# Crossbar DMA transposes of whole row blocks issued from ScalarE, in place of TensorE transposes of x and half-block transposes from SP

## The chip, the core and the metric

The kernel runs on one core of one Trainium2 chip. The metric is the device time of one execution in microseconds (us). The span of a profiled execution is some 2 us shorter than its time (1463.0 of 1464.76 us before). Several executions were timed for each kernel, and comparisons use the fast ones alone. A single-core run has no second die to compare with, so a run is called slow when it is over 1.5% above the fastest of the same kernel.

## The reference, cut to what matters

x has 8 batches, 4224 tokens and 192 channels. A causal convolution of seven taps along the tokens is followed by a token and channel mixer:

```python
theta = x @ w_theta
zr, zi = x * cos(theta), x * sin(theta)
y = einsum('ts,bsd->btd', w_tok_r, zr) + einsum('ts,bsd->btd', w_tok_i, zi)
u = x + y
out = u + maximum(u @ w_ch, 0)
```

The two 4224 x 4224 token matrices are nearly all of the work. The kernel makes the two 192 x 192 channel products (`x @ w_theta`, `u @ w_ch`) from x and u with channels on the partitions, so it transposes both. These transposes are what the change is about.

## The kernel before: the parts that the change touches

The 4224 source tokens lie in 33 chunks of 128. A step makes two blocks of 128 output tokens from the 11 chunks (9 or 10 at times) that are in memory, with seven Strassen-like runs of big matmuls for the pair. Partial sums of the outputs go to DRAM and come back one pass later. Everything is placed by hand: an event has a position in its step, counted in runs, called units here (about 3.6 us each).

Chunks 0 to 10 are prepared at the start. Chunks 11 to 21 and 22 to 32 are prepared inside running steps, one or two in a step; I call these the chunk steps of the first and second pass. The last 17 steps finish the outputs.

```python
def crossed(u):                        # crossbar transpose by DMA, half a block, from SP
    uT = turned()                      # [P, 6, P] float16, 4 buffers
    nc.sync.dma_start(out=uT, in_=u, transpose=True)
    return uT

def transposed(u, by_dve=False):       # six 128x128 transposes on TensorE, copied out of PSUM
    tp = banks("tp", F16)
    for k in range(6):
        pe(nc.tensor.transpose(tp[:, 0, k*P:(k+1)*P], u[:, k*P:(k+1)*P], ident))
    uT = turned()
    evacuate(...)                      # ScalarE (VectorE for a few)
    return uT

# Chunk.tasks: conv, conv, transpose, transpose, theta, theta, product, product, sums, sums
pos = [0, .5, 1.3, 1.6, 2.1, 2.5, 3.1, 3.15, 3.4, 3.6]     # units; the second chunk 2.3 later

# output rows: cast u to float16 (ScalarE), transpose (crossbar; TensorE in the last steps), mix
every, turn, mix = 3.6, 1.7, 9.0                            # us
```

GpSimd issues the loads of weights and x, which change float32 to float16 on the way (the software queue, q0: 163616 packets in the page of the kernel before). SP issues the partial sums in 6144-byte packets, the stores of x and the outputs (q1: 109648 packets).

## Time and profile before

| | before |
|---|---|
| time, median of the runs beside the changed kernel | 1470.94 us (1464.91 to 1472.31, 4 runs) |
| span of the profiled run | 1463.0 us |
| TensorE busy / idle | 1418.8 / 44.2 us |
| granted TensorE clock, mean | 0.998 |
| TensorE's waits for transposed x / u | 0 / 6.2 us |

TensorE is busy nearly all the time, so time is lost only where it waits, and gained only where it has less to do. The two windows below, from the windows view of the kernel before, hold the chunk steps of both passes. Their columns: window, length, busy us and instructions of PE, PEld, DVE, ACT and POOL, granted clock, DMA share, GB/s.

```profile
400.00:640.00 240.00, 239.27 (x1747) 150.18 (x1746) 172.86 (x195) 72.96 (x92) 66.85 (x119) 1.00 0.98 225
860.00:1110.00 250.00, 247.02 (x1819) 156.33 (x1818) 189.34 (x208) 77.54 (x98) 76.15 (x116) 1.00 0.96 211
```

TensorE is idle for 0.7 us in the first window and 3.0 us in the second. The DMA share is near 1, but shares of packets that overlap add up, so 1 isn't a ceiling of this share: the prediction shows a stretch of 1.16.

### The profile page before, as it was taken

The numbers are of one execution on the slowest core, as the hardware profiler recorded it, in microseconds if no ns is written. First come the engines' busy times: TensorE is split into PE (matmuls) and PEld (weight loads), VectorE is DVE, ScalarE is ACT, GpSimd is POOL, SyncE is SP. The second block draws the span as 40 slices with busy tenths as digits, with TensorE's granted clock in tenths as the row PEclk, the third lists the DMA queues.
The fourth block names the chain that finished last, engine by engine and source line by source line (L and its number), as shares of the span: only waits on it lengthen the run. The fifth ranks groups of instructions, "written<-read, shape, count | busy, mean of one in ns | idle before, by whom it ended". The sixth has DMA issues, their size and how long they took to land.

```text
span 1463.0 us, 23889 instructions
## 1 busy us (share of the span) xinstructions
PE 1418.8 (97%) x9807; PEld 886.8 (61%) x9807; DVE 992.6 (68%) x1050; ACT 324.2 (22%) x413; POOL 429.2 (29%) x659
## 2 busy tenths in 40 slices
PE   7889999999999999999999999999999999998997
PEld 4556666666666666666666656666566666665565
DVE  6884645454548687766666657877787788776676
ACT  6861111111124254000000005346001100110134
POOL 7422211111223332211112233232233343454210
PEclk9999999999999999999999999999999999999999
DMA  9976757474699999977779989999899999999994
GB/s 172 217 167 147 143 97 152 88 152 94 133 236 222 213 244 250 199 212 153 217 152 227 227 174 238 192 222 251 178 207 214 224 224 217 221 265 234 223 216 139
DMA packets 273374, 283.57 MB, mean 194 GB/s; under 512 B 107504, under 2 KB 241008, under 8 KB 273264
## 3 DMA queue, kind: packets, MB, share of 16 engines
q0 software_dynamic: 163616, 95.30, 49.0%
q1 hardware_dynamic: 109648, 186.75, 40.2%
q8 instruction: 77, 1.26, 0.3%
q14 instruction: 33, 0.27, 0.1%
HBM read 245.49 MB, written 111.28 MB: 244 GB/s over the span
## 4 chain that ended last, share of the span: by engine, by line
PE 80%; DVE 8%; DMA 5%; ACT 3%; issue 2%; POOL 0%; SPq 0%; DVEq 0%; ACTq 0%; POOLq 0%
PE y L417 72%; PE v L138 5%; DVE pv L382 2%; ACT z L242 2%; DVE wt L317 2%; DVE wt L329 2%; DMA out_dram<-pv 1%; PE pc L205 1%; PE tp L162 1%; DVE pv L446 1%; DMA uT<-ub 1%; DVE z L253 1%; DMA xw<-in_x_dram 1%; DVE z L247 1%; DMA st<-in_moe_w_tok_r_dram 1%
## 5 line engine op out<-in xcount | busy, mean ns | idle before, releaser
L417 PE MATMUL y<-z,wt 128*128 128x384 f16 x7656 | 1289.4, 326 | 10.9 <-DVE pv L382 10.0
L417 PEld LDWEIGHTS <-wt 128*128 128x128 f16 x7656 | 739.7, 98 | 485.6 <-issue 15.2
L382 DVE TENSOR_TENSOR pv<-y,pv 128x768 f32<-128x768 f32 x324 | 308.2, 952 | 362.3 <-PE y L417 333.9
L317 DVE STREAM_TRANSPOSE wt<-st 128x1408 f16<-128x1408 f16 (+7 forms) x224 | 326.4, 1462 | 26.6 <-PE y L417 19.7
L304 POOL DMA_DIRECT2D st<-in_moe_w_tok_i_dram x232 | 132.6, 580 | 496.8 <-DVE wt L317 463.3
L304 POOL DMA_DIRECT2D st<-in_moe_w_tok_r_dram x232 | 133.6, 598 | 436.4 <-DVE wt L317 421.2
L329 DVE TENSOR_TENSOR wt<-wt 128x1408 f16<-128x1408 f16 (+7 forms) x216 | 196.1, 908 | 21.8 <-PE y L417 18.2
L148 ACT ACTIVATE z<-pc 128x768 f16<-128x768 f32 x65 | 52.9, 813 | 386.6 <-PE pc L205 386.5
L436 ACT ACTIVATE ub<-pv 128x768 f16<-128x768 f32 x66 | 53.7, 838 | 349.7 <-DVE pv L382 271.8
L380 ACT ACTIVATE pv<-y 128x768 f32<-128x768 f32 x66 | 53.6, 813 | 281.6 <-PE y L417 281.6
L138 PEld LDWEIGHTS <-uT 128*128 128x128 f16 x1056 | 91.0, 98 | 32.3 <-issue 8.8
L192 POOL DMA_DIRECT2D xw<-in_x_dram x132 | 76.2, 586 | 34.4 <-DMA st<-in_moe_w_tok_r_dram 10.9
L446 DVE SCALAR_TENSOR_TENSOR pv<-v,pv 128x768 f32<-128x768 f32 x66 | 62.3, 946 | 27.6 <-PE v L138 20.9
L148 ACT ACTIVATE uT<-tp 128x768 f16<-128x768 f16 x79 | 63.3, 813 | 65.9 <-PE tp L162 65.9
L253 DVE TENSOR_TENSOR z<-z 128x768 f16<-128x768 f16 x132 | 73.3, 555 | 3.8
L364 POOL TENSOR_TENSOR pv<-pv,xr 128x1536 f32<-128x1536 f32 x20 | 62.8, 3138 | 30.6 <-DMA xr<-xs 22.2
L242 ACT ACTIVATE z<-v,half_pi 128x768 f16<-128x768 f32 x66 | 59.5, 902 | 41.7 <-PE v L138 41.6
L247 DVE TENSOR_TENSOR z<-z 128x1536 f16<-128x1536 f16 x66 | 60.3, 949 | 11.7 <-ACT z L242 11.7
L138 PE MATMUL v<-wch,uT 128*128 128x192 f16 x528 | 54.3, 246 | 8.6 <-DMA uT<-ub 6.2
L138 PE MATMUL v<-wth,uT 128*128 128x192 f16 x528 | 55.0, 248 | 3.1 <-ACT z L242 3.0
L242 ACT ACTIVATE z<-v 128x768 f16<-128x768 f32 x66 | 53.1, 805 | 0.0
L162 PE MATMUL tp<-ident,z 128*128 128x128 f16 x396 | 33.0, 220 | 8.5 <-ACT z L242 8.0
(43 smaller groups left out, 157.3 us busy)
## 6 DMA issues: line engine op xcount, KB each, us to landing
part<-pv SPq DMA_DIRECT2D x79, 768.0 KB, 4.3
pv<-part SPq DMA_DIRECT2D x79, 768.0 KB, 5.6
out_dram<-pv SPq DMA_DIRECT2D x66, 384.0 KB, 5.9
st<-in_moe_w_tok_r_dram POOLq DMA_DIRECT2D x136, 176.0 KB, 6.2
st<-in_moe_w_tok_i_dram POOLq DMA_DIRECT2D x136, 176.0 KB, 4.9
xs<-z SPq DMA_DIRECT2D x132, 96.0 KB, 4.6
xw<-in_x_dram POOLq DMA_DIRECT2D x121, 96.0 KB, 6.1
part<-xs POOLq DMA_DIRECT2D x26, 384.0 KB, 8.8
```

Source lines behind the costliest of these rows:

```text
L138: pe(nc.tensor.matmul(v[:, k, b * D : (b + 1) * D], lhsT=tT[:, 3 * k + b + i, :], rhs=w[:, 2 * b + i, :], start=(i == 0), stop=(i == 1),))
L148: act(nc.scalar.activation(out=out, in_=in_, func=AT.Copy))
L192: nc.gpsimd.dma_start(out=self.xw[lo : lo + n, h, :, :], in_=x[:, t0 : t0 + n, :].rearrange("b s d -> s b d"),)
L242: act(nc.scalar.activation(**args))
L247: dve(nc.vector.tensor_tensor(out=o, in0=xv, in1=o, op=ALU.mult))
L253: dve(nc.vector.tensor_tensor(out=z[:, o, :], in0=z[:, a, :], in1=z[:, b, :], op=ALU.subtract))
L304: pool(nc.gpsimd.dma_start(out=st[a * Q : (a + 1) * Q, 0:nb, :, 0:n] .rearrange("i r bt s -> i (r bt) s"), in_=w[self.tbs[0] * P : (self.t ...
L317: dve(nc.vector.transpose(self.w[name][:, 0 : self.n, :, :], self.st[int(name[1])][:, int(name[0]) - 1, :, 0 : self.n * Q] .rearrange("p b ...
L329: dve(nc.vector.tensor_tensor(out=self.w[name][:, 0 : self.n, :, :], in0=self.w[a][:, 0 : self.n, :, :], in1=self.w[b][:, 0 : self.n, :, : ...
L382: dve(nc.vector.tensor_tensor(out=o, in0=yv, in1=o, op=ALU.add))
L417: pe(nc.tensor.matmul(y[cn][:, q, 0:BH], lhsT=self.w[wn][:, c, :, :].rearrange("p bt i -> p (bt i)"), rhs=chunks[k].z[:, zn, q * BH : (q + ...
L446: dve(nc.vector.scalar_tensor_tensor(out=ub, in0=channel_mix(self.uT[i, g], wch), scalar=0.0, in1=ub, op0=ALU.max, op1=ALU.add,))
```

## The change

The intent: take the transposes of chunks 11 to 32 off TensorE, issue all crossbar transposes for whole blocks (128 x 1536) from ScalarE right behind the copies that make their source, and give them more time by placing theta later.

```diff
     def turned():
-        return wk.tile([P, 6, P], F16, name="uT", tag="uT", bufs=4)
+        return wk.tile([P, 12, P], F16, name="uT", tag="uT")
-    def crossed(u):
-        uT = turned()
-        nc.sync.dma_start(out=uT, in_=u, transpose=True)
+    def crossed(uT, u, by_sp=False):
+        if by_sp:
+            nc.sync.dma_start(out=uT, in_=u, transpose=True)
+        else:
+            act(nc.scalar.dma_start(out=uT, in_=u, transpose=True))
 ...
+        def cross(self):
+            self.xT = turned()
+            crossed(self.xT, self.x, self.k < NW)
 ...                                    # Chunk.tasks
-            for g in range(NG):
-                yield lambda g=g: self.transpose(g)
+            yield self.cross
 ...
-            return wpool.tile([P, NW, NQ, Q], F16, name="wt", tag="wt", bufs=10)
+            return wpool.tile([P, NW, NQ, Q], F16, name="wt", tag="wt", bufs=9)
 ...                                    # outputs of the steps that are not the last
-                    at = (8.5 if i else 0.9 - self.time / 7) if self.pair else 0.7
-                    every, turn, mix = 3.6, 1.7, 9.0
+                    at = (4 if i else 0.9 - self.time / 7) if self.pair else 0.7
+                    for g in range(NG):
+                        found.append((at + g, lambda i=i, g=g: self.cast(i, g)))
+                        found.append((at + 10.5 + 2.8 * g, lambda i=i, g=g: self.output(i, g)))
+                    found.append((at + 2, lambda i=i: self.cross_u(i)))
 ...                                    # places of a chunk's tasks
-                pos = [0, .5, 1.3, 1.6, 2.1, 2.5, 3.1, 3.15, 3.4, 3.6]
+                pos = [0, .4, .9, 4, 4.4, 5, 5.05, 5.25, 5.45]
-                at += 2.3
+                at += 0.9
```

More of the change, by code (lines that the diff above doesn't have):

```diff
@@ L150, in turned, with transposed @@
     def turned():
-        return wk.tile([P, 6, P], F16, name="uT", tag="uT", bufs=4)
-    def crossed(u):
-        uT = turned()
-        nc.sync.dma_start(out=uT, in_=u, transpose=True)
-        return uT
-    def transposed(u, by_dve=False):
+        return wk.tile([P, 12, P], F16, name="uT", tag="uT")
[4 more added lines that the diff above has]
+            act(nc.scalar.dma_start(out=uT, in_=u, transpose=True))
+    def transposed(uT, u, by_dve=False):
         tp = banks("tp", F16)
@@ L164, in transposed @@
             ))
-        uT = turned()
-        evacuate(uT[:, :, :].rearrange("p k s -> p (k s)"), tp[:, 0, 0 : 6 * P], by_dve)
-        return uT
+        evacuate(uT.rearrange("p k s -> p (k s)"), tp[:, 0, 0 : 6 * P], by_dve)
     Z11, T1, Z21, Z22, T2, T4, T3 = range(7)
@@ L175, in __init__ @@
             self.k = k
-            self.xT = {}
             self.xw = wk.tile([2 * WR, 2, B, D], F16, name="xw", tag="big", bufs=6)
@@ L226, in transpose @@
         def transpose(self, g):
-            self.xT[g] = transposed(
-                self.x[:, g * GC : (g + 1) * GC], 0 < self.k < 3 or (self.k, g) == (0, 1)
-            )
+            if g == 0:
+                self.xT = turned()
+            transposed(
+                self.xT[:, 6 * g : 6 * g + 6, :], self.x[:, g * GC : (g + 1) * GC],
+                0 < self.k < 3 or (self.k, g) == (0, 1),
+            )
+        def cross(self):
+            self.xT = turned()
+            crossed(self.xT, self.x, self.k < NW)
         def theta(self, g):
-            v = channel_mix(self.xT[g], wth).rearrange(
+            v = channel_mix(self.xT[:, 6 * g : 6 * g + 6, :], wth).rearrange(
                 "p k (b h e) -> p k b h e", b=2, h=2
@@ L434, in cast, with cross_u @@
         def cast(self, i, g):
-            self.ub[i, g] = wk.tile([P, GC], F16, name="ub", tag="ub", bufs=2)
+            if g == 0:
+                self.ub[i] = wk.tile([P, N], F16, name="ub", tag="ub", bufs=2)
+                self.uT[i] = turned()
+            cols = slice(g * GC, (g + 1) * GC)
             act(nc.scalar.activation(
-                out=self.ub[i, g], in_=self.pv[i][:, g * GC : (g + 1) * GC], func=AT.Copy
+                out=self.ub[i][:, cols], in_=self.pv[i][:, cols], func=AT.Copy
             ))
         def turn_u(self, i, g):
-            self.uT[i, g] = (transposed if self.late else crossed)(self.ub[i, g])
+            transposed(
+                self.uT[i][:, 6 * g : 6 * g + 6, :], self.ub[i][:, g * GC : (g + 1) * GC]
+            )
+        def cross_u(self, i):
+            crossed(self.uT[i], self.ub[i])
         def output(self, i, g):
@@ L446, in output @@
             dve(nc.vector.scalar_tensor_tensor(
-                out=ub, in0=channel_mix(self.uT[i, g], wch), scalar=0.0, in1=ub,
+                out=ub, in0=channel_mix(self.uT[i][:, 6 * g : 6 * g + 6, :], wch), scalar=0.0, in1=ub,
                 op0=ALU.max, op1=ALU.add,
@@ L459, in outputs @@
             for i in range(len(self.tbs)):
-                if self.late:
-                    at = 1.2 if i or not self.pair else 0.6 - self.time / 7
-                    every, turn, mix = 2.0, 1.2, 3.6
-                else:
-                    at = (8.5 if i else 0.9 - self.time / 7) if self.pair else 0.7
-                    every, turn, mix = 3.6, 1.7, 9.0
+                if not self.late:
+                    at = (4 if i else 0.9 - self.time / 7) if self.pair else 0.7
+                    for g in range(NG):
+                        found.append((at + g, lambda i=i, g=g: self.cast(i, g)))
+                        found.append((at + 10.5 + 2.8 * g,
+                                      lambda i=i, g=g: self.output(i, g)))
+                    found.append((at + 2, lambda i=i: self.cross_u(i)))
+                    continue
+                at = 1.2 if i or not self.pair else 0.6 - self.time / 7
+                every, turn, mix = 2.0, 1.2, 3.6
                 for g in range(NG):
```

## The prediction

> **What bounds the kernel now.** I read the page first (parts 1, 2, 4 and 5), then the engines in 50 us windows, then the timeline of one step in which later chunks of x are prepared, then who the TensorE waited for, then the DMA view.
>
> ```profile
> PE 1418.8 (97%) x9807; PEld 886.8 (61%) x9807; DVE 992.6 (68%) x1050; ACT 324.2 (22%) x413; POOL 429.2 (29%) x659
> L417 PE MATMUL y<-z,wt 128*128 128x384 f16 x7656 | 1289.4, 326 | 10.9 <-DVE pv L382 10.0
> L148 ACT ACTIVATE uT<-tp 128x768 f16<-128x768 f16 x79 | 63.3, 813 | 65.9 <-PE tp L162 65.9
> L162 PE MATMUL tp<-ident,z 128*128 128x128 f16 x396 | 33.0, 220 | 8.5 <-ACT z L242 8.0
> ```
>
> The TensorE is busy for 1418.8 of 1463.0 us, so only 44 us are idle, and about 20 of those lie in the first 100 us, which the change leaves alone. Whatever takes work off the TensorE shortens the kernel, unless a wait takes its place. The transposes of x (L162, 396 of them = 66 half blocks of six) are such work. ScalarE, at 22%, is not a bound.
>
> The busy times of short matmuls overlap their neighbours, so I take their real cost from the starts in the timeline of the TensorE:
>
> ```profile
> 454.57 0.65 PE L417 MATMUL y<-z,wt 128*128 128x384 f16 x3
> 455.06 0.50 PE L162 MATMUL tp<-ident,z 128*128 128x128 f16 x6
> 455.39 1.14 PE L417 MATMUL y<-z,wt 128*128 128x384 f16 x6
> 456.37 0.50 PE L162 MATMUL tp<-ident,z 128*128 128x128 f16 x6
> 456.70 0.33 PE L417 MATMUL y<-z,wt 128*128 128x384 f16 x1
> ```
>
> Six transposes hold the array for 455.39 - 455.06 = 0.33 us (again 456.70 - 456.37), not for the 0.50 us shown as busy. A big matmul takes (456.37 - 455.39)/6 = 0.163 us. So a half block costs 0.33 us, or 55 ns a transpose.
>
> The waits of the TensorE between 1300 and 1400 us, and the windows of a chunk step, a plain step, a final step and a stretch near the end (columns: length, busy us of PE, PEld, DVE, ACT, POOL with counts, clock, DMA share, GB/s):
>
> ```profile
> PE v L138 <- DMA uT<-ub: 6.2, 5, 2.1
> 441.50:468.20 26.70, 26.70 (x217) 17.22 (x216) 22.36 (x27) 12.66 (x16) 9.10 (x16) 1.00 1.04 235
> 650.00:675.00 25.00, 25.00 (x156) 15.07 (x154) 16.17 (x16) 0.00 (x0) 4.55 (x8) 1.00 0.77 184
> 1089.00:1117.20 28.20, 27.84 (x189) 17.71 (x187) 22.12 (x20) 3.26 (x4) 10.84 (x11) 1.00 1.03 219
> 1312.00:1360.00 48.00, 42.27 (x286) 26.43 (x284) 29.72 (x31) 4.11 (x5) 24.08 (x28) 1.00 1.16 226
> ```
>
> The chunk steps and most final steps have a full TensorE; only around 1312 to 1360 us is time lost (5.7 us), nearly all of it to crossbar transposes of u that land late. VectorE is at 22.36/26.70 = 84% in a chunk step, and the DMA share is already about 1.0 there.
>
> [...] In this trace a TensorE transpose inside a stream costs 55 ns, so I use that. [...] on SP a transpose issued at 1083.34 us moved its first packet only at 1086.74, while 6144-byte packets of a partial-sum transfer were passing. [...]
>
> **The change part by part.**
> (a) x of the chunks 11 to 32. Removed from the TensorE: 22 chunks x 2 half blocks x 0.33 us = 14.5 us. All of it lies in windows where the TensorE is 100% busy (about 430 to 590 and 880 to 1050 us), so it comes off the end one for one. ScalarE loses 44 copies of 0.81 us and gains 22 DMA issues. An issue of half a block took 1.25 us on SP, so I estimate 2.5 us for a whole one: 36 us less, 55 us more, at an idle engine. The PSUM buffers that the next convolution and theta need are two deep, and no more than one is held up behind an issue, so I charge nothing.
> (b) Does the transpose land in time? It is placed 0.9 and theta 4.0 units of a step (a seventh, some 3.6 us) after the chunk's start: 3.1 x 3.6 = 11.2 us. In the packet records a half-block transpose is 768 packets of 256 bytes, 18 ns each undisturbed; alone it spans 0.9 us from first to last packet, beside other queues 2 to 2.7 us in the 1077 to 1260 us stretch. The first packet comes 1.2 us after the issue. For a whole block: copy and semaphore 1, first packet 1.2, 1536 packets 2 to 6 us, so 4 to 8 us, under 11.2. Charge: 0, with some risk of 1 or 2 us in a few chunks.
> (c) DMA load. 1536 x 18 ns / 16 = 1.7 us of all engines per chunk; 11 chunks in about 155 us add 0.12 to the share of 1.0. The stretch from 1312 us ran at 1.16, and there transfers were late; the one from 1089 ran at 1.03 without waits for transfers. Weights and partial sums are asked for some 20 us ahead, so I charge 1 us.
> (d) The VectorE bunches. Before, the products and sums of a step's two chunks stood at 3.2 to 3.7 and 5.5 to 6.0 units; now at 5.1 to 5.55 and 6.0 to 6.45. A chunk takes two products and four sums, by starts in the timeline 1.74 + 2.24 = 4.0 us. From unit 5.0 the VectorE has: addition of the fifth product 0.88, weight sum 0.67, chunk 4.0, addition of the sixth 0.88, chunk 4.0, addition of the seventh 0.88 = 11.3 us. The last must be done when run 0 of the next step ends, at unit 8.0, 3.0 x 3.55 = 10.65 us later, for the accumulator is reused then. It misses by some 0.6 us. The kernel before shows this wait in one such bunch:
>
> ```profile
> 496.70 3.57 PE L417 MATMUL y<-z,wt 128*128 128x384 f16 x21 [0.73 <-DVE pv L382]
> ```
>
> There are five two-chunk steps in each of two passes: 10 x 0.6 = 6 us lost.
> (e) u. 48 half-block transposes on SP become 24 whole ones on ScalarE, which no longer queue behind the transfers of SP. Their distance from the first cast to the first use grows from 9.0 to 10.5 us, but the first half now waits for the whole. Undisturbed steps had no wait and gain nothing. Near the end the half blocks' packets spanned 4 to 6.5 us each beside accumulating transfers, so a whole block (2 us until it is issued, 1.2, then 8 to 10) is still late by 1 to 2 us there, two or three times. Of the 6.2 us lost I expect 3 to come back.
> (f) One weight tile fewer. Counting live tiles through a step (seven in use, freed one per run; eight made), the most is nine, reached at units 2.2, 3.05, 3.3, 4.2 and 5.1, each just after a run has freed one. The VectorE has waited for that run anyway. Charge 0.
> Sum: -14.5 + 1 + 6 - 3 = -10.5 us on 1463, so 0.7%. On the median 1470.62 that is 1460; since the runs before scatter from 1464.91 to 1471.26 with the median at the upper end, I put 1458.
>
> **The rivals.** (1) No new wait: the VectorE slips by less than I worked out and all late transposes vanish. Then -14.5 - 6 - 2 = -22 us, about 1446. For it: the margin in (d) is a difference of nearly equal numbers. Against: 84% VectorE already. (2) The crossbar transpose of x becomes the wait: at a DMA share of 1.13, whole blocks take 10 us or more, theta waits 1 or 2 us in each of 22 chunks (theta's slack is 3 to 7 us), so 22 to 40 us are lost against 14.5 gained: 1475 to 1490. For it: the bursts of 4 to 6.5 us near the end. Against: those stood beside accumulating transfers, which chunk steps lack. (3) The saved array time is hidden, because a step is paced by the VectorE (84%, 88% after a step shortened to 25.4 us): gain only 2 to 4 us, about 1467. For it: (d). Against: a queue at 88% with one run of slack follows most of the shortening.
>
> **Range and chances.** Rival 1 sets the low edge, rival 3 with a mild form of 2 the high one: 1445 to 1471. Over 2% faster would need 29 us, more than the 14.5 + 6.2 us plus the small VectorE waits on offer: 4%. Over 2% slower needs rival 2 in full: 3%. Within 2%: 93%.
>
> **What would show each step right or wrong.** L162 down from 396 to 132 on z, PE busy down by 14 to 22 us (22 because busy time counts overlap): (a). TensorE waits on the transposed x near zero: (b); several us in total: rival 2. TensorE waits for L382 in the chunk windows near 6 us: (d); near 0: rival 1. Waits of v for the transposed u at 2 to 4 us after 1300: (e). VectorE waits for the TensorE at the weight tiles unchanged near 20 to 40 us: (f). Chunk steps about 1.3 us shorter, or 0.7 with the waits of (d). What would make all of it wrong is a wait on ScalarE's sequencer, which now issues DMAs between copies: if an issue blocks it for far over 2.5 us, convolutions and sines stand behind it.

Its sum came to -10.5 us (-14.5 + 1 + 6 - 3).

## The result, and the profile after

The changed kernel takes 1561.93 us (median of 4 runs, 1543.7 to 1571.47), against 1470.94. The ratio is 1.0536, with a 95% interval of 1.0461 to 1.0611. Ratios here are the mean time of one kernel's fast runs over that of the other's in the same rounds, so they are not quite the ratio of the medians quoted. The kernel became 5% slower where a gain of 1% had been predicted. It also scatters more: two of its four runs are over 1.5% above its fastest and count as slow. The profiled run (1553.38 us, span 1551.3) is a fast one.

First the page of the changed kernel, which answers the lines in the prediction (L421 is the old L417):

```profile
PE 1431.6 (92%) x9543; PEld 884.2 (57%) x9543; DVE 1006.9 (65%) x1050; ACT 289.4 (19%) x369; POOL 430.3 (28%) x659
...
PEclk9999999999999999999999988998999999988999
...
L138 PE MATMUL v<-wth,uT 128*128 128x192 f16 x528 | 59.7, 261 | 43.1 <-DMA uT<-z 40.6
L138 PE MATMUL v<-wch,uT 128*128 128x192 f16 x528 | 56.2, 251 | 31.6 <-DMA uT<-ub 30.0
```

The view of groups shows the transposes left of x:

```profile
L163 PE MATMUL tp<-ident,z 128*128 128x128 f16 x132 | 11.7, 230 | 8.2 <-ACT z L247 7.6 <-ACT z L148 0.5
```

The work did leave TensorE: 396 transposes of x became 132. Yet its busy time rose, from 1418.8 to 1431.6 us, and its idle time rose from 44.2 to 119.7 us. The row PEclk, the granted clock in tenths, has new dips in the columns where the idle time is. The waits of TensorE in the changed kernel (total us, times, longest):

```profile
PE v L138 <- DMA uT<-z: 40.6, 8, 11.1
PE v L138 <- DMA uT<-ub: 30.0, 7, 15.4
PE y L421 <- DVE pv L386: 10.9, 11, 3.6
...
PE pc L203 <- DMA xw<-xw: 6.2, 5, 2.9
PE pc L203 <- DMA xw<-in_x_dram: 5.9, 3, 3.1
```

and the one of VectorE before:

```profile
PE y L417 <- DVE pv L382: 10.0, 15, 1.8
```

70.6 us are waits for transposes, where the kernel before had 6.2. Another 12.1 us are waits of the convolution for the loads of x. The wait for VectorE, from which I had expected the main loss, hardly moved. The same windows as above, with one near the end:

```profile
400.00:640.00 240.00, 216.19 (x1477) 131.73 (x1475) 160.63 (x182) 57.00 (x71) 64.61 (x114) 0.97 1.10 224
860.00:1110.00 250.00, 217.06 (x1440) 131.58 (x1439) 160.16 (x182) 52.98 (x67) 64.03 (x112) 0.92 1.06 198
1360.00:1410.00 50.00, 34.61 (x216) 21.52 (x215) 24.31 (x24) 3.15 (x4) 16.32 (x18) 0.83 1.20 191
```

TensorE issues fewer matmuls in the same windows and gets a clock of 0.83 to 0.97. What that means for one matmul is seen in the timelines just after a wait, first the weight loads:

```profile
452.38 0.15 PEld L421 LDWEIGHTS <-wt 128*128 128x128 f16 x1 [0.17 <-issue]
452.69 0.15 PEld L421 LDWEIGHTS <-wt 128*128 128x128 f16 x1 [0.17 <-issue]
453.01 0.15 PEld L421 LDWEIGHTS <-wt 128*128 128x128 f16 x1 [0.17 <-issue]
```

and the matmuls, eight in a row each:

```profile
450.80 1.46 PE L138 MATMUL v<-wth,uT 128*128 128x192 f16 x8 [7.59 <-DMA uT<-z]
452.05 2.67 PE L421 MATMUL y<-z,wt 128*128 128x384 f16 x8
```

After a wait of 7.59 us the big matmuls follow each other every 0.32 us instead of 0.163. The clock records of the trace agree: they show 12 stretches at exactly half clock between 100 and 1500 us, of 3.41 to 17.07 us and all whole multiples of 3.41 us, all at waits of about 3 us and more (12 of the 13 waits of 2.88 us or more are followed by one); the kernel before has none between 100 us and its last matmul.

This gives the account of the 88.3 us between the two spans. TensorE's idle time grew by 119.7 - 44.2 = 75.5 us. The overlap of the half-clock stretches with busy TensorE time is 50.8 us, half of which, 25.4 us, is lost. The transposes saved 14.5 us. Together 75.5 + 25.4 - 14.5 = 86.4 us; some 2 us are left over.

By stage, I take the times from the start of the 2000th big matmul to that of the 3200th (it holds the first pass's chunk steps), from the 4700th to the 6000th (the second pass's), and from there to the end:

| span, us | first pass | second pass | end |
|---|---|---|---|
| before | 230.1 | 257.4 | 334.7 |
| after | 252.6 | 298.8 | 357.2 |
| loss | 22.5 | 41.4 | 22.5 |

Between these stages the two kernels are alike (243.8 us both), and the first 2000 matmuls take 1.9 us longer after.

Lateness shows in the view of the transposed tile, between 890 and 1090 us of the changed kernel (durations of an issue in ns, then issue to landing):

```profile
L158 ACTq DMA_TRANSPOSE uT<-z x11: 1383/1678/6583, 900.9 to 1067.2; - x11
...
DMA to landing us min/median/max: 3.2/7.4/21.2
```

I had allowed 11.2 us. In the packet records, the 1536 packets of one whole-block transpose of x span between 1.55 and 16.22 us. The two shortest (1.55 and 1.77 us) have no packets of the software queue beside them. The longest, issued at 905.38 us, has 1647 data packets of that queue and 128 of 6144 bytes beside it. Issuing can block ScalarE's sequencer as well, as this timeline near the end shows:

```profile
1373.59 19.09 ACTq L158 DMA_TRANSPOSE uT<-ub  x1
1394.41 1.46 PE L138 MATMUL v<-wch,uT 128*128 128x192 f16 x8 [15.39 <-DMA uT<-ub]
```

One issue holds ScalarE's sequencer for 19.09 us, until just after the transpose before it has landed (its last packet ends at 1391.16).

### The profile page after: what moved, and what is told of

Its sections match the earlier page's. It is cut to its first block, busy times and chain, and to the rows that moved or that the text cites. A ratio compares the mean times of both kernels' runs of the same rounds, so it can differ in the third digit from the quotient of the medians.

```text
span 1551.3 us, 23231 instructions
## 1 busy us (share of the span) xinstructions
PE 1431.6 (92%) x9543; PEld 884.2 (57%) x9543; DVE 1006.9 (65%) x1050; ACT 289.4 (19%) x369; POOL 430.3 (28%) x659
## 3 DMA queue, kind: packets, MB, share of 16 engines
q10 hardware_dynamic: 72128, 18.09, 10.1%
## 4 chain that ended last, share of the span: by engine, by line
PE 69%; DMA 18%; DVE 7%; ACT 4%; issue 2%; POOL 0%; SPq 0%; ACTq 0%; DVEq 0%
PE y L421 62%; DMA uT<-z 7%; DMA uT<-ub 5%; PE v L138 5%; DVE pv L386 2%; DMA st<-in_moe_w_tok_r_dram 2%; DMA xw<-in_x_dram 2%; ACT z L247 1%; DMA xw<-xw 1%; DVE z L252 1%; PE pc L203 1%; DVE z L258 1%; DVE wt L333 1%; DVE pv L458 1%; DVE wt L321 1%
## 5 line engine op out<-in xcount | busy, mean ns | idle before, releaser
L421 PE MATMUL y<-z,wt 128*128 128x384 f16 x7656 | 1298.7, 329 | 11.8 <-DVE pv L386 10.9
L421 PEld LDWEIGHTS <-wt 128*128 128x128 f16 x7656 | 747.4, 99 | 501.9 <-issue 27.7
L321 DVE STREAM_TRANSPOSE wt<-st 128x1408 f16<-128x1408 f16 (+7 forms) x224 | 327.5, 1465 | 42.5 <-PE y L421 36.2
L333 DVE TENSOR_TENSOR wt<-wt 128x1408 f16<-128x1408 f16 (+7 forms) x216 | 204.1, 945 | 45.9 <-PE y L421 43.4
L138 PEld LDWEIGHTS <-uT 128*128 128x128 f16 x1056 | 94.9, 102 | 99.3 <-DMA uT<-z 43.6
L138 PE MATMUL v<-wth,uT 128*128 128x192 f16 x528 | 59.7, 261 | 43.1 <-DMA uT<-z 40.6
L203 PE MATMUL pc<-xw,bands 96*64 96x192 f16 x528 | 38.1, 260 | 14.1 <-DMA xw<-xw 6.2
L203 PEld LDWEIGHTS <-bands 96*64 96x64 f16 x528 | 22.7, 112 | 35.5 <-issue 26.8
```

Of the source, the lines that this page charges most:

```text
L138: pe(nc.tensor.matmul(v[:, k, b * D : (b + 1) * D], lhsT=tT[:, 3 * k + b + i, :], rhs=w[:, 2 * b + i, :], start=(i == 0), stop=(i == 1),))
L203: pe(nc.tensor.matmul(pc[half * 2 * Q : (half + 1) * 2 * Q, h // 2, h % 2 * B * G : (h % 2 + 1) * B * G], lhsT=bands[:, 4 * j + h, :, :].r ...
L321: dve(nc.vector.transpose(self.w[name][:, 0 : self.n, :, :], self.st[int(name[1])][:, int(name[0]) - 1, :, 0 : self.n * Q] .rearrange("p b ...
L333: dve(nc.vector.tensor_tensor(out=self.w[name][:, 0 : self.n, :, :], in0=self.w[a][:, 0 : self.n, :, :], in1=self.w[b][:, 0 : self.n, :, : ...
L421: pe(nc.tensor.matmul(y[cn][:, q, 0:BH], lhsT=self.w[wn][:, c, :, :].rearrange("p bt i -> p (bt i)"), rhs=chunks[k].z[:, zn, q * BH : (q + ...
```

## The experiments

The theories at the start: **A**, the crossbar's small packets take turns with those of the other queues on each DMA engine, so a transpose is late wherever those are busy, whichever queue issues it; **B**, ScalarE's own ring is at fault ("ring" and "row" here and in the expectations mean a queue of the page: in the changed kernel q10 with 72128 packets holds the transposes from ScalarE, beside SP's q1 and the software queue q0); **C**, x alone overloads the DMA engines and u suffers from it; **D**, the whole block is at fault, since theta's first half waits for all of it. After the first four runs **L** came in: the chunk steps have no room left on the DMA engines. By each packet's undisturbed duration, an estimate from the trace's shortest packets of each size, 0.88 of the engines' time is taken between 450 and 560 us of the kernel before, and the transposes of x add 0.12.

The six runs marked "one run" among the kernels were executed once, so their state is unknown, and near-copies of the changed kernel scatter from 1543.7 to 1592.54 us. From single runs I therefore read waits and packets more than the time.

### Parts of the change: u alone and x alone

u_alone: whole-block transposes of u from ScalarE stay, x goes back to TensorE.

```diff
-            yield self.cross
+            for g in range(NG):
+                yield lambda g=g: self.transpose(g)
-                pos = [0, .4, .9, 4, 4.4, 5, 5.05, 5.25, 5.45]
+                pos = [0, .5, 1.3, 1.6, 2.1, 2.5, 3.1, 3.15, 3.4, 3.6]
-                at += 0.9
+                at += 2.3
```

> x of all chunks by TensorE again, at its old places in the step; u in whole blocks from ScalarE as in the changed kernel. The parts of the loss are read from the changed kernel's trace. Theory A (the crossbar's small packets take turns with the packets of the software queue and of SP, so a transpose is late wherever those are busy): the u part stays: the 30 us that TensorE waited for u against 6 before, and some 12 us of half clock after the long waits, so about 1495 us. Theory B (ScalarE's own ring is at fault): the same, about 1495. Theory C (only x overloads the DMA engines, and u is late as a consequence of that): near 1465.

Measured: correct, 1486.26 us (median of 4), ratio 1.0099 (1.0048 to 1.015). The stages are 230.1, 257.2 and 354.9 us: the passes are as before, the end is 20.2 us longer. TensorE waits 26.6 us for u, all of it in three waits between 1285 and 1372 us (the longest 15.8), where the kernel before lost 6.2. So C falls: u is late on its own account. The unchanged passes also show that nine weight tiles cost nothing.

x_alone: x as in the change, u again in half blocks from SP at the old places.

```diff
+                crossed(*half, by_sp=True)      # in turn_u, half a block
-                    at = (4 if i else 0.9 - self.time / 7) if self.pair else 0.7
+                    at = (8.5 if i else 0.9 - self.time / 7) if self.pair else 0.7
+                    every, turn, mix = 3.6, 1.7, 9.0
```

> u in half blocks from SP at its old places again (its cast still goes into a whole-block tile); x by crossbar from ScalarE as in the changed kernel. Theories A and B: the waits for x (40 us), those for the x windows (12 us) and some 20 us of half clock stay, less the 14.5 us of transposes: about 1518 us. Theory C: about 1540, nearly the whole loss.

Measured: correct, 1540.36 us (median of 4), ratio 1.0509 (1.0455 to 1.0563), which is more than A and B expected. Stages 248.9, 307.9, 339.1. TensorE waits 51.1 us for x. The transposes of x make most of the loss, those of u about 20 us, and the two nearly add up. (The transposes from ScalarE end at 1083.71 us and those from SP begin at 1121.66, so the two queues never transpose at the same time here.)

### The ring and the size: all_sp and halves

all_sp issues every crossbar transpose from SP (`if by_sp:` becomes `if True:`).

> The changed kernel with every crossbar transpose issued from SP instead of ScalarE, same sizes and places. Theory B (own ring, starved by turns): the transposes' packets span 2 to 5 us again and the time falls to about 1460. Theory A (turns with the software queue, on either ring): the packets of the late ones still span 8 us or more, and SP's queue adds its own waiting: 1530 to 1580 us.

Measured: correct, 1532.88 us (one run; before 1468.38). Stages 244.9, 300.1, 343.5. The spans of the x transposes' packets fall to 1.6 to 7.4 us, but the first packet comes 1.2 to 6.6 us after the issue (1.2 to 4.8 us in the change). In the kernel before, where SP issues them too, other packets of SP went first: the transpose issued at 1083.34 us had its first packet at 1086.74. TensorE waits 48.7 us for x, in 14 waits of up to 7.0 us. B falls as an explanation of the time: without the ring of its own the spans are shorter but the first packet comes later, and the wait for x (40.6 us in the change) is no less. B did foresee the shorter spans, and A's "8 us or more" was too high there.

halves gives each whole-block transpose as two half-block ones, both from ScalarE:

```diff
-            crossed(self.xT, self.x, self.k < NW)
+            for g in range(NG):
+                crossed(self.xT[:, 6*g : 6*g+6, :], self.x[:, g*GC : (g+1)*GC])
```

(and the same for u).

> The changed kernel with each whole-block transpose given as two half-block ones, one after the other, from ScalarE. Theory D (the whole block is at fault: theta's first half waits for all of it): the waits for x and u fall by more than half, about 1500 us. Theory A: the packets are the same and take the same turns; the first half comes some 4 us earlier but the second is needed only 1.5 us after the first, so the waits fall by a quarter at most: 1530 to 1550 us.

Measured: correct, 1501.41 us (one run). D met its number, and A, which had asked for 1530 to 1550 us, missed. But look at TensorE's waits in this run:

```profile
PE pc L203 <- DMA xw<-in_x_dram: 13.3, 7, 3.8
PE pc L203 <- DMA xw<-xw: 12.4, 10, 3.2
...
PE v L138 <- DMA uT<-z: 4.9, 5, 1.8
```

The wait for the transposed x shrinks from 40.6 to 4.9 us, and that for the loads of the next chunks' x doubles from 12.1 to 25.7. What lands late changed. Stages 241.8, 278.5, 337.1: nearly all of u's loss is gone, and about half of the loss in the two passes stays (11.7 + 21.1 us). The turns themselves are as many as A had them: while the transposes of x ran, 8389 data packets of the software queue and 822 of 6144 bytes went by (7803 and 787 in the change). But they are spread otherwise, and the longest time from a chunk's first issue to its last packet fell from 20.5 to 12.5 us. So a part of the loss goes with the size of the block; whether by the earlier first half or by the shorter worst case, this run doesn't tell.

### Nobody waits for the transposes: dummy

The kernel before, with 22 whole-block transposes in the places of the change that nobody reads:

```diff
+    def unread():
+        dst = wk.tile([P, 12, P], F16, name="dT", tag="xr", bufs=2)
+        act(nc.scalar.dma_start(
+            out=dst, in_=wboth.rearrange("p a d -> p (a d)"), transpose=True))
 ...
+                n_x = sum(1 for j in range(NW, k) if start[j] == start[k])
+                found.append((1.0 + 0.9 * n_x, unread))
```

(`wboth` holds the two channel matrices, 1536 columns; nine weight tiles.)

> The kernel before (x and u as there) plus 22 whole-block crossbar transposes that nobody reads, issued from ScalarE where the changed kernel issues those of x; source and target are tiles that nothing else uses at that time, one weight tile fewer as in the change. Theory L (in the chunk steps the DMA engines have no room left: by undisturbed packet times 0.88 of their time is taken before, and the transposes of x add 0.12): other transfers come late, above all the loads of x for the next chunks, though no instruction waits for a transpose: 1485 to 1520 us. Theory A (only the lateness of the transposes themselves costs): 1463 to 1472 us.

Measured: correct, 1587.61 us (one run; before 1463.7): slower than the change itself and than either theory had it. TensorE still does all transposes of x here and no instruction reads the new ones. In the waits view:

```profile
ACT z L242 <- issue: 86.5, 8, 19.6
...
PE v L138 <- ACT z L242: 66.3, 15, 17.7
```

and in the timeline, where the issue of a transpose stands before ScalarE's next sine:

```profile
468.55 16.50 ACTq L481 DMA_TRANSPOSE dT<-wboth  x1
...
485.10 0.90 ACT L242 ACTIVATE z<-v,half_pi 128x768 f16<-128x768 f32 x1 [15.20 <-issue]
```

The issue takes 16.50 us, and the sine that theta needs stands behind it, so TensorE waits for ScalarE. The semaphore that this issue waits for had its last update at 463.6 us, before the issue began, so the 16.50 us are no wait for a semaphore. This is a second way in which late transposes cost: ScalarE's sequencer is held for as long as an issue takes. In the change it costs little at x, where theta needs the transpose anyway (the longest issue there is 6.58 us). Because of this, dummy doesn't measure the load alone, and L can't be read from it.

### Less traffic: lighter, quiet, no_w

lighter leaves out the stores of partial sums in the chunk steps of the second pass: `if not self.final and not 35 <= self.t <= 40:`.

> The changed kernel with the stores of partial sums left out in the chunk steps of the second pass (steps 35 to 40; wrong results on purpose), which takes away 0.14 of the DMA engines' time there. The first pass is the control and should lose what it lost before (some 25 us of idle TensorE between 430 and 610 us). Theory L: in the second pass TensorE's idle time falls from 34 us (gaps over 1 us between 900 and 1080 us) to under 10. Theory A: the transposes still take turns with the software queue's packets, so at least 20 us stay.

Measured: wrong output, 1540.38 us (one run). Stages 245.8, 290.9, 359.2. The first pass, whose code is that of the change, differs from the change's own profile by 6.8 us, so the 7.9 us by which the second is shorter tell nothing. The windows view for the second pass:

```profile
860.00:1110.00 250.00, 214.81 (x1454) 130.96 (x1453) 160.09 (x182) 55.76 (x70) 62.01 (x109) 0.94 0.98 166
```

The rate fell from 198 to 166 GB/s, and TensorE is as idle as before (250 - 214.81 = 35.2 us against 32.9). L, which asked for gaps under 10 us, missed its forecast. But the DMA share of this window is still 0.98 (1.06 in the change), so the run shows only that leaving out the stores is not enough; it doesn't show that there was room.

quiet was to move the first weight load of a chunk step from 1.3 to 3.4 units, away from the transposes.

> The changed kernel with the first weight load of a chunk step moved from 1.3 to 3.4 units, away from the two transposes of x, nothing taken away. Theory A: the second transposes span 3 to 5 us instead of 8 to 16, waits for x fall from 40 us to under 15, time about 1510. Theory L: the same bytes in the same step; the waits move to other transfers and the time stays at 1535 to 1560.

Measured: correct, 1592.54 us (one run). Neither theory was tested, because the edit did not do what I meant. In the timeline the load is issued at 430.45 us against 431.65 in the change: in both, the idle time of GpSimd before it (12.43 and 12.41 us) was ended by VectorE, which frees the weight buffer, so moving the event did not put the load later. As a nearly unchanged copy the run shows instead how widely such a kernel scatters (1543.7 to 1592.54 us with the change's own runs).

no_w leaves out the weight loads of steps 35 to 42 (issued two steps earlier, so in all chunk steps of the second pass) and uses those of step 34:

```diff
+            if 35 <= self.t <= 42:
+                self.st[m] = steps[self.t - 1].st[m]
+                return
```

> The changed kernel with the weight loads of steps 35 to 42 left out, the weights of step 34 used instead (wrong on purpose): in the steps of the second pass that prepare x, but the last two, the software queue carries only x. The first pass is the control (some 25 us of gaps). Theory A: the second transposes of a step in the second pass span under 6 us instead of 11 to 16 and their waits (24 us between 900 and 1080 us) fall under 5, until the last step or two. If they stay late, taking turns with the weights is not the cause.

Measured: wrong output, 1498.08 us (one run). Its windows view for the first pass (control) and the second:

```profile
400.00:640.00 240.00, 216.72 (x1463) 131.83 (x1462) 159.71 (x182) 56.63 (x71) 63.81 (x112) 0.95 1.11 224
860.00:1110.00 250.00, 245.02 (x1698) 150.88 (x1696) 189.47 (x208) 58.85 (x74) 41.91 (x65) 0.99 0.79 188
```

The control loses 23 us of TensorE as in the change, the second pass 5. There the waits for transposed x are under 1 us in all (24.4 in the change) and the packets span 1.6 to 4.9 us. The stage takes 253.4 us, 4 us less than before the change. So beside x's own loads and all partial sums the change works as it was meant, and beside the weight loads it does not. That is A's forecast. (It takes away bytes too, some 0.33 of the engines' time, as I estimate from the undisturbed durations of the packets; lighter had taken 0.14 without effect, so this pair alone does not exclude a threshold.)

### The cost by itself: micro and micro2

A kernel of its own has phases in which everything is waited for in between: one whole-block transpose alone, or beside weight loads as the kernel issues them, 768 KB loads of partial sums, or both.

> The disputed cost by itself (output wrong on purpose): a whole-block crossbar transpose (1536 packets of 256 bytes) in phases with everything waited for in between: from ScalarE alone; beside two weight loads of the software queue; beside four 768 KB loads of partial sums on SP; beside both; then beside both as two halves, from SP behind its loads, none, and whole from ScalarE and from SP again. Theory A (each DMA engine serves one packet of each row with work in turn): per engine 96 turns, of 18 ns alone, 18+74 beside weights, 18+234 beside sums, 18+74+234 beside both, as long as the neighbours last: spans 1.7 us alone, about 8.8 beside weights, about 9 beside the sums (their 32 packets an engine last 32 turns, 8 us), 12 to 18 beside both; halves the same in sum; from SP it starts only after the loads (8 us or more) and then spans under 9. Theory L (bytes alone count): beside both the transpose ends only 2 us later than alone plus its share, under 6 us.

Measured: 322.66 us, mostly inconclusive. The software queue's first packets come 4 us after the start of a phase, and by then the transposes from ScalarE had ended: 2.00 us from first to last packet alone, 2.00 and 2.01 beside neighbours that had not begun. Later phases overlapped only in part. In micro2, ScalarE therefore copies for some 8 us first, and there are more loads:

```diff
+            for _ in range(5):
+                nc.scalar.activation(out=slow, in_=zero, func=AT.Copy)
+            nc.scalar.activation(out=src, in_=slow, func=AT.Copy)
             cross(nc.scalar, halves)
```

> In micro the transposes had run before the neighbours' transfers began (4 us after the issue), so most phases told nothing. Here ScalarE copies for about 8 us before it issues the transpose, the weight loads are sixteen (some 20 us) and the sums eight, so that the transpose runs amid them (output wrong on purpose). Phases: alone; beside weights; beside sums; beside both; both, as halves; from SP behind four of the sums, weights running; both; weights; sums; both without a transpose. Theory A (one packet of each row in turn): spans 2.0 us alone (as micro showed); 96 x (18+74) = 8.8 us beside weights; 96 x (18+234), cut off when the sums end, so 10 us or more beside sums; more than beside either when beside both, 15 us or more; from SP it starts late and then spans about 8.8. Theory L (room alone): under 5 us beside one neighbour, since neither fills the engines.

Measured (504.35 us for the whole, output wrong), from the packet records:

| phase | span of the 1536 packets | packets of the others in it |
|---|---|---|
| alone | 2.00 us | none |
| beside weights | 8.17 us | 1643 of the weights |
| beside both | 21.86 us | 1639 of the weights, 896 of the sums |
| both, as two halves | 21.86 us | 1682 and 896 |
| weights again | 9.88 us | 1354 |

The DMA view of the window of the second phase says the same (queue, packets, MB, share of the 16 engines; 1536 packets of data and 32 small ones make 1568):

```profile
q0 software_dynamic: 1782, 1.18, 93.5%
q10 hardware_dynamic: 1568, 0.39, 35.5%
```

and of the third, where the partial sums (q1) come in:

```profile
q1 hardware_dynamic: 1008, 5.51, 66.2%
q0 software_dynamic: 1783, 1.18, 36.9%
q10 hardware_dynamic: 1566, 0.39, 11.5%
```

Against A's forecast of 8.8 us beside weights stand 8.17 and 9.88; against "15 us or more" beside both stand 21.86. For each of its 1536 packets about one of the weights' goes by (1643), although they are nearly three times as large. Halves do not change the sum, as A had it. L's "under 5 us" is refuted, and so is its premise that one neighbour doesn't fill the engines: just before the transpose of the second phase began, the weights alone moved 254 packets per us, at a DMA share of 1.26. With the transpose there, between 78 and 84 us, 194 weight packets and 206 of the transpose went by per us. So the transpose did not get what was left over; the weights gave way. Beside both, between 136 and 153 us, the counts per us are 52 of the weights, 49 of the sums and 55 of the transpose, though their packets have 704, 6144 and 256 bytes. In this stretch the three queues shared by packets, and not by bytes. It wasn't always so even: "weights again" met 1354 weight packets, and another phase meant to be beside both met 1047 of the weights, only 37 of the sums, and took 10.50 us. The phases beside sums alone missed the overlap (11 and 9 sum packets), and the transpose from SP ended before the weight loads began, so these say nothing.

The real kernels show the same order. I sorted the half-microseconds within the transposes' spans of six runs with whole blocks from ScalarE (after, u_alone, x_alone, dummy, quiet, lighter) by whether any data packet of the software queue or of SP's queue starts in them. The transposes move 797 packets per us where there is neither, 278 where there are some of the software queue, 330 where there are some of SP, and 119 where there are both. At these mean rates 1536 packets take 1.9, 5.5, 4.7 and 12.9 us.

### Two tries to beat both: first_only and first_v2

first_only transposes only the first new chunk of a step by crossbar (two halves from ScalarE), the second on TensorE, u as before:

```diff
+            if self.by_crossbar:
+                yield self.cross
+            else:
+                for g in range(NG):
+                    yield lambda g=g: self.transpose(g)
+                chunks[k].by_crossbar = at < 0.5
-                at += 0.9
+                at += 0.6
```

> Meant to beat both: u in half blocks from SP as before; of x only the first (or only) new chunk of a step by crossbar, in two half blocks from ScalarE, the second by TensorE. Takes 12 x 2 x 0.33 = 7.9 us off TensorE and adds 0.065 to the DMA engines' share, to 0.94. Theory L: just fits, few waits: 1456 to 1466 us, ratio 0.993 to 1.000. Theory A: the first transposes of a step landed in 2 to 4 us in the changed kernel too, so no waits: 1458.

Measured: correct, 1490.95 us (median of 4), ratio 1.0179 (1.0157 to 1.02). One transpose in 12 came late (8.5 us). TensorE's waits for VectorE doubled to 19.9 us, because my placement put VectorE's work on the two chunks side by side.

first_v2 puts the TensorE chunk where the kernel before has it, and theta of the crossbar chunk at 2.6 units (`pos = [0, .4, .9, 2.6, 3, 3.6, 3.65, 3.9, 4.1]`, `at += 2.3`).

> A second try to beat both: the first new chunk of a step by crossbar in two halves from ScalarE, theta 2.6 units after the start; the second chunk by TensorE exactly where the kernel before has it, so that VectorE's work of the two chunks is as far apart as before; u as before. In first_only the loss was the bunching on VectorE (20 us of waits against 10) and one late transpose. Theory A: the first transposes run before the weights of the step are asked for, so they land in 4 to 6 us of 6.5: at best -7.9 us, 1456 to 1463; with a few waits and half-clock stretches 1465 to 1475.

Measured: correct, 1536.15 us (median of 6), ratio 1.0482 (1.0433 to 1.053). The waits for VectorE are down to 8.6 us, but TensorE waits 50.9 us for transposed x, in 13 waits. With the slack cut to 1.7 units, second halves that span 8 to 9 us beside partial sums and weights are late. Neither version beats the kernel before, and I know of none in this family that would: even with no weight loads at all, a pass gained 4 us.

## Why the prediction was wrong, point by point

**(a)** was right: TensorE does 264 transposes fewer, and the account above closes, to 2 us, with 14.5 us saved. The 2.5 us for an issue hide a long tail: the median for x was 1.84 us, but 10 of 22 took over 2.5 us, up to 6.58.

**(b)** is the step that failed. It said that a whole block's packets need "2 to 6 us", so 4 to 8 us to landing, and charged nothing. I had read that from half blocks in a stretch where the software queue was mostly quiet, and doubled it. Measured: 2.00 us alone, but 8.17 to 9.88 beside weight loads and 21.86 beside weights and sums; in the changed kernel landing took up to 21.2 us of the 11.2 allowed. A better estimate stood within reach in the same records: 96 packets per engine, each with a 74 ns weight packet before it and at times a 234 ns sum packet (undisturbed durations), instead of 96 x 18 ns. The kernel before even has a half block beside weight packets: the one issued at 1283.44 us took 4.16 us for its 768 packets, with 759 packets of 704 bytes and only 10 of the sums among them, and 0.9 us is its undisturbed span.

**(c)** had the load about right (the DMA share rose from 0.98 to 1.10 in the first pass's window) and its consequence wrong: 12.1 us of waits for the loads of x instead of 1 us.

**(d)** did not occur: TensorE's waits for VectorE went from 10.0 to 10.9 us, not up by 6. Lateness elsewhere may have hidden it; first_only, where these waits were 19.9 us, shows that the bunching can cost.

**(e)** had the wrong sign: +20.2 us in u_alone instead of -3. That the transposes "no longer queue behind the transfers of SP" was to take a wait away, and this was the fault. From ScalarE their first packets came 1.2 to 16.2 us after the issue (median 3.36), from SP before 1.2 to 8.3 us (median 3.37). Where all three queues were busy they shared the engines (52, 49 and 55 packets per us in micro2), and in whole blocks the first half waits for the second. all_sp shows that issuing from SP costs too: 48.7 us of waits for x.

**(f)** was right in cost, as u_alone's unchanged passes show. VectorE's waits for weight tiles doubled (19.7 + 18.2 to 36.2 + 43.4 us) but did not reach TensorE.

**Rival 2** was the right picture, at 3%: whole blocks of 10 us and more, against waits of 1 or 2 us each on which I based its price. What I held against it, that the late half blocks near the end stood beside accumulating transfers, is not so for the one at 1283.44 us: no accumulating packet runs beside it. It also lacked a term that no part of the prediction had: after 12 of the 13 waits of 2.88 us or more TensorE ran at half clock, which added 25.4 us to 75.5 us of idle time. A wait on TensorE here costs about a third more than its length.

What stays open: micro2 shows full engines shared by packets (52, 49 and 55 per us), but not how much of the loss in the kernel would go if the same packets met engines with more room, which no_w and lighter don't separate; and what remains late in the halves run, where the loads of x take the place of the transposes.

## What to carry to other kernels

Before moving work from a full TensorE to DMA, count packets and not bytes. In micro2 a transfer of 1536 small packets met 1643 packets of the busy weight queue and took 8.17 us instead of 2.00, and 21.86 us beside both queues. So, as an estimate, multiply the packets per engine by the sum of the undisturbed packet times, the transfer's own and one of each busy neighbour (96 x (18 + 74) ns = 8.8 us here), in the stretch where it will really run. Compare that with the slack to its first reader. Price a miss at more than its length: in the change the array's clock was halved after 12 of the 13 waits of 2.88 us or more, which added 25.4 us to 75.5 us of idle time. Don't let an engine issue such transfers if later work on that engine is needed soon: an issue held ScalarE for 16.50 us in dummy, and its sequencer for 19.09 us in the change.
